# Reordering the start of the last stage of a fused attention and expert kernel, folding weights in three rounds, and swapping operands for its last token block

## The chip, the core and the metric

The kernel runs on one core of one Trainium2 chip. The metric is the device time of one execution in microseconds (us), the median of several executions. The engines are named as the profile names them: PE is TensorE (PEld its weight loads), ACT ScalarE, DVE VectorE, POOL GpSimd, and SP the queue that issues all transfers.

## The reference

Attention over 4 batches, 12 heads, 448 tokens and 64 columns gives `x` with 1792 rows (tokens) and 768 columns. A soft mixture of experts makes 32 slots out of all tokens, sends them through 8 small networks, and mixes the slot outputs back into every token. The last stage multiplies by one more pair of matrices with `h * cos(h)` between them.

```python
d = softmax over tokens of x @ phi          # 1792 x 32
slot_input = d.T @ x                        # 32 x 768
slot_out[e] = relu(slot_input[e] @ w1[e]) @ w2[e]
x2 = c @ slot_out                           # c: softmax over slots, 1792 x 32
h = x2 @ w_in                               # 768 x 2048, float64 numbers
out = (h * cos(h)) @ w_out                  # 2048 x 768, float64 numbers
```

## The kernel before, in words

The front part (attention, then the slots) takes the first half of the time and is the same instruction for instruction before and after. At its end come the slot outputs: groups of matmuls whose 256 result columns ACT copies from PSUM into `so`, PE transposes, and DVE copies into `soT` (the tile `dT` in the trace).

The last stage never forms `x2`. It cuts the 2048 inner columns into 16 chunks and, for each, **folds** the slot outputs into the weight chunk: `w_mm` (task `wm`, six matmuls of 128 columns a chunk, one for each 128 rows of `soT`, each written to one of four strips of 32 output partitions), `w_4` (ACT copies), `w_rep` (task `wr`, one matmul that adds the strips up), `w_s` (ACT) and `w_d` (task `wd`, DVE). `GRP` says which one or two chunks share a fold. The weights arrive as float64; each 768 KB load goes into one of four raw buffers and is **decoded** into float32 by four instructions: `dec_a` on ACT (task `a`) and `dec_l`, `dec_h`, `dec_s` on DVE (`l`, `h`, `s`). Loads are numbered j = 0, 1, 2, ... (even: `w_in`, odd: `w_out`); load j takes the raw buffer of load j - 4 and is issued (`ld`) when `s` of j - 4 is done. A chunk of `w_out` is then split into a high part (task `u`, ACT) and a remainder (task `v`, POOL or DVE).

The tokens are cut into three blocks of 512 and a last one of 256 columns. A **step** s is one pair of block and chunk; `SEQ` lists the 64 of them, the last block being the last 16. A step is a chain: `H` (PE, one matmul into bank 6 or 7), `Y` (ACT), `R` (DVE), `S` (ACT, sine), `G` (DVE, which frees the bank), `K` (ACT, high part), `L` (POOL, remainder), and then `B`: for each of six 128-row pieces of the output three product matmuls into that piece's own PSUM bank, with weights stationary and activations moving:

```python
o = bank[m][:, 0:n_(s)]
PE.matmul(o, lhsT=wh, rhs=gh, start=first, stop=False)
PE.matmul(o, lhsT=wl, rhs=gh, start=False, stop=False)
PE.matmul(o, lhsT=wh, rhs=gl, start=False, stop=last)
```

Step 0 runs its 18 products in three passes of six (`back0`): high weights first, then the weight remainder, then the activation remainder. At a block's last chunk `finish` (task `F`) copies or adds the bank into SBUF and, at chunk 15, issues the store.

What runs when is set by a planner in the kernel's own code: each of the tasks above has a duration, dependencies and a key; a list scheduler with these numbers writes out one fixed order per engine, and every engine then works strictly in that order. Matmuls on a constant tile (`keep_warm`, each two records of 128 columns) fill PE's order where the planner sees it idle before the first product.

Of the kernel before, what the change touches and what calls it, by code (L numbers as in the profile page):

```python
# [8 lines left out]
F32 = mybir.dt.float32  # L9
# [22 lines left out]
SAFE = 0.0  # L32
LA = .4
KD = 0.0
LD = False
KW = (0, 7, 2, 2)
PL = {23: 2, 24: 1}
CFG = {'rm': 2,
        'evx': 'D',
# [117 lines left out]
def moe_stack_kernel(ctx: ExitStack, tc: tile.TileContext, qk, v, cst, phi, w1, w2, w_in, w_out, out):  # L157
# [505 lines left out]
    def w_cols(c, u):  # L663

        if c < 12:
            return [(ar[f"hl{c}"], 768 * u, 0, 6)]
        t = [ar[f"hl{3 * (c - 12) + i}"] for i in range(3)]
        return [(t[0], 1536, 0, 4), (t[1], 1536, 4, 2)] if u == 0 else [(t[1], 1792, 0, 2), (t[2], 1536, 2, 4)]

# [95 lines left out]
    with tc.manual_schedule():  # L765
        for g in range(2):
# [115 lines left out]
    def back0(s, m):  # L882
# [3 lines left out]
        for m in range(6):  # L886
            fc = seq[0][1]
            PE.matmul(bank[m][:, 0:n_(0)], lhsT=w_blk(fc, int(k_ == 1), m), rhs=gl if k_ == 2 else gh, start=k_ == 0,
                      stop=k_ == 2 and seq[0][3])

    def finish(s, m, eng):
        blk, fc = seq[s][:2]
        o, ob = bank[m][:, 0:n_(s)], part(blk, m)[:, 0:n_(s)]
        if any(t[0] == blk and t[3] for t in seq[:s]):
            DVE.tensor_tensor(ob, o, ob, ALU.add)
        elif eng is DVE:
            DVE.tensor_copy(ob, o)
        else:
            ACT.activation(ob, o, AF.Copy)
        if fc == 15:  # L900
            SP.dma_start(out[128 * m:128 * m + 128, TOK[blk]:TOK[blk + 1]], ob)

# [29 lines left out]
    task(("so",), dict(DMA=5.199999999999999), [], -1)  # L932
    for q, grp in enumerate(GRP):
        key = need[grp[0]] - 1.5
        n = len(grp)
        task(("wm", q), dict(T=.3 + .45 * n), [("s", 2 * c) for c in grp if c] + [("w4", q - 2) if q >= 2 else None, ("so",)], key - .8)
# [4 lines left out]
    pb = {}  # L941
    for s, (blk, fc, first, last) in enumerate(seq):
        w = n_(s) / 512.0
# [4 lines left out]
        task(("G", s), dict(D=.07 + .54 * w), [("S", s)], s - 2.3)  # L948
        task(("K", s), dict(A=.1 + .46 * w), [("G", s), ("B", s - 4, 5) if s >= 4 else None], s - 1.7)
# [5 lines left out]
        for m in range(6):  # L955
            if s == 0:
# [3 lines left out]
                continue  # L960
            pv_ = ("B", s, m - 1) if m else (("B", s - 1, 5) if s else None)
            task(("B", s, m), dict(T=.01 + .67 * w), [("K", s), ("L", s), ("u", fc), ("v", fc), pv_, pb.get(m) if first else None], s + m / 10)
            if last:
                seen = any(t[0] == blk and t[3] for t in seq[:s])
                task(("F", s, m), dict(D=.07 + .54 * w) if seen or m % 2 == 0 else dict(A=.08 + .42 * w), [("B", s, m)], s + .2 + m / 10)
                pb[m] = ("F", s, m)
    LAT = dict(T=.24, A=.17, D=.1, P=.1, DMA=.9)
# [100 lines left out]
    with tc.manual_schedule():  # L1068
        for _, _, t, e in plan:
# [75 lines left out]
```

## Time and profile before

| | before |
|---|---|
| median of 3 runs | 527.82 us (527.72 to 528.99) |
| the profiled execution's own time | 532.41 us |
| span in the profile, first to last instruction | 530.6 us |
| PE, DVE, ACT, POOL busy | 498.8, 351.2, 310.5, 184.3 us |
| granted TensorE clock, mean | 0.986 of full speed |

The span is 1.8 us shorter than the profiled execution, and that execution is 4.6 us longer than the median of the runs without a profiler. The slot outputs end, and the last stage begins, near 248 us of the span. A matmul row's duration is longer than the distance to the next one's start, since matmuls overlap; what PE needs for one is read from start to start.

### The profile page before, as it was taken

Reading aid. Unit: us, or ns where it says so; the run is one execution under the profiler, and the core shown is the slowest. Engines: PE = TensorE matmul, PEld = TensorE weight load, DVE = VectorE, ACT = ScalarE, POOL = GpSimd, SP = SyncE. Lnnn points to the kernel's source line nnn. Section 1 sums busy time; section 2 is a strip of 40 time slices with the busy share of each in tenths; the row PEclk is TensorE's granted clock in tenths of the full one; section 3 lists DMA queues with packets and bytes.
Section 4 is the critical chain, followed back from the end, with each engine's and each line's share of the span. In section 5 each row is a group of like instructions: output and inputs, shape, how many; then the busy total and the mean of one; then the engine's idle time right before and its main releaser. Section 6 shows DMA issues by size and latency. Waiting matters only on the chain.

```text
span 530.6 us, 11216 instructions
## 1 busy us (share of the span) xinstructions
PE 498.8 (94%) x4292; PEld 364.7 (69%) x4292; DVE 351.2 (66%) x874; ACT 310.5 (59%) x734; POOL 184.3 (35%) x251
## 2 busy tenths in 40 slices
PE   6999999999999898886889999999999999999997
PEld 4676577576666633243767868787877777888996
DVE  3788688778767452003888899887997976445431
ACT  3899789779868121002769665747556546543552
POOL 0565356435445000000326333243434357222321
PEclk9899999989989999999899999999999999999999
DMA  5596767748658899999453423333163010213101
GB/s 193 176 324 225 272 216 254 256 164 299 210 179 319 309 416 422 421 419 417 160 192 107 153 86 119 120 117 122 63 225 105 26 61 24 95 40 131 69 1 61
DMA packets 24246, 100.38 MB, mean 189 GB/s; under 512 B 2816, under 2 KB 6912, under 8 KB 18048
## 3 DMA queue, kind: packets, MB, share of 16 engines
q1 hardware_dynamic: 24192, 99.66, 51.3%
q8 instruction: 34, 0.56, 0.4%
q14 instruction: 20, 0.16, 0.1%
HBM read 94.14 MB, written 5.51 MB: 188 GB/s over the span
## 4 chain that ended last, share of the span: by engine, by line
PE 55%; DVE 17%; DMA 16%; ACT 8%; issue 2%; POOL 1%; SPq 0%; ACTq 0%; POOLq 0%; DVEq 0%
PE bank L377 10%; PE bank L880 7%; PE bank L879 7%; PE bank L878 7%; PE bank L295 7%; DMA w<-in_w_dram 6%; PE bank L333 6%; DMA zraw<-in_w_out_dram 5%; DMA zraw<-in_w_in_dram 4%; DVE zscr L859 2%; ACT zraw L704 2%; DVE zscr L865 2%; ACT zscr L862 2%; PE bank L852 2%; DVE zhl L739 2%
## 5 line engine op out<-in xcount | busy, mean ns | idle before, releaser
L878 PE MATMUL bank<-zg,zhl 128*128 128x512 f32 (+1 forms) x378 | 139.7, 370 | 0.4 <-ACT zhl L726 0.4
L879 PE MATMUL bank<-zg,zhl 128*128 128x512 f32 (+1 forms) x378 | 137.5, 364 | 0.9 <-DVE zhl L739 0.9
L880 PE MATMUL bank<-zg,zhl 128*128 128x512 f32 (+1 forms) x378 | 137.3, 363 | 0.8 <-POOL zg L871 0.8
L871 POOL TENSOR_TENSOR zg<-zscr,zg 128x512 fp32r<-128x512 f32 (+1 forms) x64 | 82.7, 1297 | 140.3 <-ACT zg L868 127.3
L330 POOL TENSOR_SCALAR p<-p,pst 128x448 f32<-128x448 f32 (+3 forms) x168 | 81.5, 505 | 89.7 <-ACT pts L179 62.0
L313 ACT ACTIVATE p<-p,pst 128x448 f32<-128x448 f32 (+3 forms) x168 | 87.4, 521 | 22.1 <-DVE pst L311 22.1
L878 PEld LDWEIGHTS bank<-zg,zhl 128*128 128x128 f32 x378 | 71.5, 189 | 13.7 <-issue 1.2
L880 PEld LDWEIGHTS bank<-zg,zhl 128*128 128x128 f32 x378 | 71.4, 189 | 12.6 <-POOL zg L871 1.3
L879 PEld LDWEIGHTS bank<-zg,zhl 128*128 128x128 f32 x378 | 71.5, 189 | 12.4 <-DVE zhl L739 1.4
L862 ACT ACTIVATE zscr<-zscr,b_h 128x512 f32<-128x512 f32 (+1 forms) x64 | 42.0, 669 | 31.4 <-DVE zscr L859 31.3
L859 DVE SCALAR_TENSOR_TENSOR zscr<-zscr,bank 128x512 f32<-128x512 int32 (+1 forms) x64 | 38.7, 617 | 32.3 <-ACT zscr L856 31.9
L311 DVE CUSTOM_DVE_ANT_0 p<-bank,cs 128x448 f32<-128x448 f32 (+1 forms) x96 | 50.7, 547 | 10.8 <-PE bank L295 10.8
L295 PE MATMUL bank<-qk 64*128 64x192 f32 (+2 forms) x288 | 55.6, 462 | 0.6 <-ACT xk L179 0.5
L868 ACT ACTIVATE zg<-zscr 128x512 fp32r<-128x512 f32 (+1 forms) x64 | 36.3, 575 | 26.0 <-DVE zscr L865 25.9
L865 DVE TENSOR_TENSOR zscr<-bank,zscr 128x512 f32<-128x512 f32 (+1 forms) x64 | 39.1, 620 | 18.3 <-ACT zscr L862 18.3
L856 ACT ACTIVATE zscr<-bank,b_q 128x512 int32<-128x512 f32 (+1 forms) x64 | 39.4, 629 | 19.2 <-PE bank L852 19.0
L739 POOL TENSOR_TENSOR zhl<-uacc,zhl 128x768 fp32r<-128x768 f32 (+1 forms) x7 | 10.8, 1552 | 99.9 <-DMA zraw<-in_w_out_dram 84.8
L704 ACT ACTIVATE zraw<-zraw 128x768 f32<-128x768 f32 x32 | 29.2, 912 | 25.7 <-DMA zraw<-in_w_in_dram 14.6
L181 DVE COPY pts<-bank 128x512 f32<-128x512 f32 x48 | 33.0, 687 | 12.3 <-PE bank L333 12.0
L333 PE MATMUL bank<-cs,p 64*128 64x64 f32 (+1 forms) x768 | 34.7, 228 | 1.3 <-POOL p L330 1.0
L333 PEld LDWEIGHTS bank<-cs,p 64*128 64x128 f32 (+1 forms) x768 | 28.6, 135 | 7.0 <-POOL p L330 3.9
L179 ACT ACTIVATE pts<-bank 128x512 f32<-128x512 f32 x48 | 28.0, 584 | 8.1 <-PE bank L333 7.6
(143 smaller groups left out, 709.2 us busy)
## 6 DMA issues: line engine op xcount, KB each, us to landing
w<-in_w_dram SPq DMA_DIRECT2D x48, 1024.0 KB, 8.0
zraw<-in_w_in_dram SPq DMA_DIRECT2D x16, 768.0 KB, 4.5
zraw<-in_w_out_dram SPq DMA_DIRECT2D x16, 768.0 KB, 4.4
qk<-in_qk_dram SPq DMA_DIRECT2D x24, 480.0 KB, 3.6
xk<-in_v_dram SPq DMA_DIRECT2D x12, 256.0 KB, 4.7
out_dram<-zps SPq DMA_DIRECT2D x8, 256.0 KB, 2.0
xts<-in_v_dram SPq DMA_DIRECT2D x12, 128.0 KB, 3.5
lt<-in_v_dram SPq DMA_DIRECT2D x12, 128.0 KB, 4.1
```

The source lines that it names most:

```text
L295: PE.matmul(sreg(j, c), lhsT=Q(p)[h, q0:q0 + 128], rhs=K(p)[h, 0:ln], start=True, stop=True)
L311: DVE.tensor_tensor_reduce(out=dst, in0=sb, in1=m, scale=-0.125, scalar=3.0e38, op0=ALU.add, op1=ALU.min, accum_out=st_[:, col:col + 1])
L313: return pr(f"exp{j}{c}")(lambda: ACT.activation(dst, dst, AF.Exp, bias=st_[:, col:col + 1], scale=-1.0, accum_out=st_[:, 8 + col:9 + col]))
L330: ENG[CFG["norm"][3 * j + c if c < 3 else 6]].tensor_scalar(dst, dst, st_[:, 24 + col:25 + col], 0.0, op0=ALU.mult, op1=ALU.add)
L333: PE.transpose(out, src, by)
L377: PE.matmul(OB[64 * j:64 * j + 64, a:b], lhsT=V(p, c, j), rhs=r[j], start=first, stop=last)
L862: ACT.activation(y_(s), y_(s), AF.Sin, bias=b_h, scale=1.0)
L865: DVE.tensor_tensor(y_(s), hb[:, 0:n_(s)], y_(s), ALU.mult)
L871: eng.tensor_tensor(g_(s)[1], y_(s), g_(s)[0].bitcast(F32), ALU.subtract)
L878: PE.matmul(o, lhsT=wh, rhs=gh, start=first, stop=False)
L879: PE.matmul(o, lhsT=wl, rhs=gh, start=False, stop=False)
L880: PE.matmul(o, lhsT=wh, rhs=gl, start=False, stop=last)
```

## The change

Four things are edited; all lie after the 248th microsecond.

- **Slot outputs first.** The copy into `so` and the copy into `soT` stand ahead of the decoding of load 1 on ACT and on DVE instead of behind it, with one more `keep_warm` ahead of the transposes and two behind the second copy.
- **Fold in three rounds.** Where a fold has two chunks, its twelve `wm` matmuls are dealt over the four strips so that no strip gets more than three; before, two strips got four.
- **Last block with activations stationary.** `back3` replaces `back` in the last 16 steps: the activations are `lhsT` (two groups of 128 tokens), the weight chunk is the moving operand, and the output is not transposed. A step's 18 matmuls of 256 columns become 6 of 512 and 6 of 256, in three units that take banks 0, 2, and 1 with 3. `finish3` replaces six copies and six stores of 128 KB by two copies of 512 columns, two of 256, and three stores of 256 KB.
- **A new order.** 52 keys of the planner are shifted (`KEYS`), three `v` tasks are put on a named engine (`VE`), and some of its durations and starting times are altered.

```diff
-LA = .4
+LA = 0.3
+KEYS = {
+    ('B', 10, 2): 7.75, ('B', 12, 5): 3.75, ('B', 13, 3): 1, ('B', 14, 3): 8.75, ('B', 18, 2): 2, ('B', 18, 4): 5.25,
...
+VE = {0: 'D', 3: 'P', 8: 'D'}
...
-                if npc[0] == 48:
-                    decode(1)
                 ACT.activation(so, sb[:, 0:256], AF.Copy)
                 tb = bank[6]
                 if npc[0] == 48:
-                    keep_warm(1)
+                    keep_warm(2)
+                    dec_a(1)
...
+                if npc[0] == 48:
+                    keep_warm(2)
+                    dec_l(1)
+                    dec_h(1)
+                    dec_s(1)
...
     def w_mm(q, wb):
-        for k_, n in enumerate(GRP[q]):
-            for ch in range(6):
-                r = ch % 4
-                PE.matmul(wb[32 * r:32 * r + 32, 128 * k_:128 * k_ + 128], lhsT=soT[:, ch, :],
-                          rhs=fwi(n)[:, 128 * ch:128 * ch + 128], start=(ch < 4), stop=(ch + 4 >= 6))
+
+        ts = [(0, 0, 0), (0, 1, 1), (0, 2, 2), (0, 3, 3), (0, 4, 0), (0, 5, 1)]
+        if len(GRP[q]) == 2:
+            ts += [(1, 0, 2), (1, 1, 3), (1, 2, 2), (1, 3, 3), (1, 4, 0), (1, 5, 1)]
+        seen = set()
+        for x, (k_, ch, r) in enumerate(ts):
+            PE.matmul(wb[32 * r:32 * r + 32, 128 * k_:128 * k_ + 128], lhsT=soT[:, ch, :],
+                      rhs=fwi(GRP[q][k_])[:, 128 * ch:128 * ch + 128], start=(k_, r) not in seen,
+                      stop=not any(y[0] == k_ and y[2] == r for y in ts[x + 1:]))
+            seen.add((k_, r))
...
+    U3 = (((0, 0, 512, 0),), ((1, 0, 512, 2),), ((0, 512, 768, 1), (1, 512, 768, 3)))
...
+    def back3(s, k):
+
+        blk, fc, first, last = seq[s]
+        gh, gl = g_(s)
+        for k_, a, b, bn in U3[k]:
+            ob = bank[bn][:, 0:b - a]
+            th, tl = (g[:, 128 * k_:128 * k_ + 128] for g in (gh, gl))
+            wh, wl = w_seg(fc, 0, a, b), w_seg(fc, 1, a, b)
+            PE.matmul(ob, lhsT=th, rhs=wh, start=first, stop=False)
+            PE.matmul(ob, lhsT=th, rhs=wl, start=False, stop=False)
+            PE.matmul(ob, lhsT=tl, rhs=wh, start=False, stop=last)
+
+    def finish3(k, eng):
+        o3 = out[DM * TOK[3]:DM * NT].rearrange("(t p c) -> p t c", t=2, p=128)
+        if k < 2:
+            ob = ar["ps"][:, 512 * k:512 * k + 512]
+            copy("D" if eng is DVE else "A", ob, bank[(0, 2)[k]])
+            SP.dma_start(o3[:, k, 0:512], ob)
+            return
+        ob = ar["ps"][:, 1024:1536]
+        DVE.tensor_copy(ob[:, 0:256], bank[1][:, 0:256])
+        ACT.activation(ob[:, 256:512], bank[3][:, 0:256], AF.Copy)
+        SP.dma_start(o3[:, :, 512:768], ob.rearrange("p (t c) -> p t c", t=2))
...
-    free = dict(T=6.0, A=5.6, D=5.95, P=3.0)
+    free = dict(T=3.6, A=3.95, D=6.05, P=3.0)
```

How the instructions stand is shown at three places; line numbers differ between the two files.

**ACT, at the end of the slot outputs.** `cs<-bank_68 128x256` is the copy into `so`, `zraw_2734` to `zraw_2737` are `dec_a` of loads 0 to 3, `cs<-bank_70` is `w_4` and `zWS` is `w_s` of the first fold. Before:

```order
L704 ACTIVATE zraw_2734<-zraw_2734 128x768
L704 ACTIVATE zraw_2735<-zraw_2735 128x768
L798 ACTIVATE cs<-bank_68 128x256
L704 ACTIVATE zraw_2736<-zraw_2736 128x768
L827 ACTIVATE cs<-bank_70 128x128
L704 ACTIVATE zraw_2737<-zraw_2737 128x768
L834 ACTIVATE zWS<-bank_70 96x128
```

and now:

```order
L714 ACTIVATE zraw_2734<-zraw_2734 128x768
L806 ACTIVATE cs<-bank_68 128x256
L714 ACTIVATE zraw_2735<-zraw_2735 128x768
L847 ACTIVATE cs<-bank_70 128x128
L714 ACTIVATE zraw_2736<-zraw_2736 128x768
L854 ACTIVATE zWS<-bank_70 96x128
```

The copy moved ahead of `dec_a` of load 1; `dec_a` of load 2 now stands between the first fold's two ACT copies.

**PE, from the second fold on.** `zfa,dT` and `zfb,dT` are `wm`, `cs 96x...` is `wr`, `CT,zWS` is `H`, `cs 128x128` is `keep_warm`, `zg,zhl` are products. Before, the second fold and `H` of steps 0 (the row just ahead), 1 and 2 all stand ahead of the first product:

```order
L852 MATMUL bank_70<-CT,zWS 128x512
L819 MATMUL bank_71<-zfa,dT 32x128 x6
L467 MATMUL bank_67<-cs 128x128 x2
L830 MATMUL bank_71<-cs 96x128
L467 MATMUL bank_67<-cs 128x128 x6
L852 MATMUL bank_70<-CT,zWS 128x512
L852 MATMUL bank_71<-CT,zWS 128x512
L888 MATMUL bank_64<-zg_3072,zhl_3075 128x512
```

Now the 18 products of step 0 come first (after 17 `keep_warm`), with `wm` of the second fold between the second and the third pass. What stands between the last of them and the first product of step 1 is this:

```order
L908 MATMUL bank_69<-zg_3075,zhl_3078 128x512
L850 MATMUL bank_70<-cs 96x128
L872 MATMUL bank_70<-CT,zWS 128x512
L872 MATMUL bank_71<-CT,zWS 128x512
L872 MATMUL bank_70<-CT,zWS 128x512
L837 MATMUL bank_71<-zfb,dT 32x128 x12
L898 MATMUL bank_64<-zg_3075,zhl_3079 128x512
```

`wr` of the second fold, `H` of steps 1, 2 and 3 and `wm` of the third fold moved from both sides into the place between step 0 and step 1.

**DVE, around `G` of step 0.** `zscr<-bank_70,zscr` is `G`, `zWS` is `wd` of the second fold, the rows on `zraw` are decoding (`TENSOR_SCALAR` is `l`, the first `SCALAR_TENSOR_TENSOR` on a load is `h`, the second `s`), `zhl` is `v`. Before:

```order
L865 TENSOR_TENSOR zscr<-bank_70,zscr 128x512
L838 TENSOR_TENSOR zWS<-bank_71,zWS 32x128
L711 SCALAR_TENSOR_TENSOR lt<-zraw_2737,lt 128x768
L859 SCALAR_TENSOR_TENSOR zscr<-zscr,bank_70 128x512
L859 SCALAR_TENSOR_TENSOR zscr<-zscr,bank_71 128x512
L707 TENSOR_SCALAR zfb<-zraw_2736 128x768
```

and now:

```order
L885 TENSOR_TENSOR zscr<-bank_70,zscr 128x512
L749 TENSOR_TENSOR zhl_3078<-uacc,zhl_3078 128x768
L725 SCALAR_TENSOR_TENSOR zfa<-zraw_2736,zfa 128x768
L717 TENSOR_SCALAR zfb<-zraw_2734 128x768
L721 SCALAR_TENSOR_TENSOR zfb<-zraw_2734,zfb 128x768
L721 SCALAR_TENSOR_TENSOR lt<-zraw_2737,lt 128x768
L725 SCALAR_TENSOR_TENSOR lt<-zraw_2737,lt 128x768
L717 TENSOR_SCALAR zfb<-zraw_2736 128x768
L858 TENSOR_TENSOR zWS<-bank_70,zWS 32x128
L725 SCALAR_TENSOR_TENSOR zfb<-zraw_2734,zfb 128x768
```

`v` of chunk 0 came from POOL to DVE, and `wd` of the second fold fell from the row behind `G` to eight rows behind it, right after `l` of load 6 (the second use of `zraw_2736`).

Farther on, `wr` of the later folds moved away from their `wm`: the third fold had 3 product matmuls between the two and has 18, the fourth had 3 and has 18, the fifth had 3 and has 45; and of the undivided `v` tasks of chunks 1 to 11 six stood on DVE before (chunks 1, 4, 6, 7, 9, 11) and three stand there now (5, 8, 11).

## Rows read from the trace of the kernel before

**Rows 1.** PE's waits from 266 us to the end: us in total, times, longest.

```profile
PE bank L852 <- DVE zscr L865: 1.7, 3, 0.9
PE bank L852 <- DVE zWS L838: 1.5, 2, 0.8
PE bank L879 <- DVE zhl L739: 0.9, 1, 0.9
PE bank L830 <- ACT cs L827: 0.9, 2, 0.5
PE bank L880 <- POOL zg L871: 0.8, 1, 0.8
```

**Rows 2.** PE's timeline, 247 to 275 us: start, us, what, idle before.

```profile
247.76 1.05 PE L792 MATMUL bank<-w,dk 128*4 128x256 f32 x16 [0.58 <-DMA w<-in_w_dram]
...
250.86 0.44 PE L803 MATMUL bank<-cs 128*128 128x128 f32 x2 [1.63 <-ACT cs L798]
252.68 1.07 PE L819 MATMUL bank<-zfa,dT 128*32 128x128 f32 x12 [1.38 <-DVE dT L804]
...
255.12 1.28 PE L467 MATMUL bank<-cs 128*128 128x128 f32 x6
256.16 0.48 PE L852 MATMUL bank<-CT,zWS 96*128 96x512 f32 x1
256.57 0.63 PE L819 MATMUL bank<-zfa,dT 128*32 128x128 f32 x12
...
257.93 1.50 PE L467 MATMUL bank<-cs 128*128 128x128 f32 x12
...
260.51 4.26 PE L888 MATMUL bank<-zg,zhl 128*128 128x512 f32 x18
...
266.80 0.50 PE L879 MATMUL bank<-zg,zhl 128*128 128x512 f32 x1 [0.94 <-DVE zhl L739]
...
273.86 1.07 PE L819 MATMUL bank<-zfb,dT 128*32 128x128 f32 x24
```

**Rows 3.** ACT's timeline, 249 to 253 us.

```profile
249.63 0.90 ACT L704 ACTIVATE zraw<-zraw 128x768 f32<-128x768 f32 x1 [8.99 <-DMA zraw<-in_w_out_dram]
250.44 0.37 ACT L798 ACTIVATE cs<-bank 128x256 f32<-128x256 f32 x1
251.52 0.95 ACT L704 ACTIVATE zraw<-zraw 128x768 f32<-128x768 f32 x1 [0.72 <-DMA zraw<-in_w_in_dram]
```

**Rows 4.** DVE's timeline, 252 to 267 us.

```profile
252.44 0.18 DVE L804 COPY dT<-bank 128x32 f32<-128x32 f32 x1
252.54 0.55 DVE L707 TENSOR_SCALAR zfa<-zraw 128x768 int32<-128x768 int32 x1
...
254.19 0.96 DVE L715 SCALAR_TENSOR_TENSOR zfa<-zraw,zfa 128x768 int32<-128x768 int32 x1
...
265.34 1.40 DVE L739 TENSOR_TENSOR zhl<-lt,zhl 128x768 fp32r<-128x768 f32 x1 [0.32 <-ACT zhl L726]
```

**Rows 5.** Stretches of 1 us: busy us of PE, PEld, DVE, ACT, POOL; then PEclk.

```profile
253.00:254.00 1.00, 1.00 (x13) 0.59 (x6) 0.90 (x2) 0.21 (x2) 0.00 (x0) 0.50 0.84 221
...
256.00:257.00 1.00, 1.00 (x16) 0.68 (x15) 0.55 (x1) 0.70 (x2) 0.55 (x1) 0.97 0.91 227
```

**Rows 6.** All 32 weight loads (line 697): issue to landing.

```profile
DMA to landing us min/median/max: 4.0/4.4/19.2
```

**Rows 7.** PE's timeline: a run of 512-column, then of 256-column products.

```profile
487.81 0.40 PE L878 MATMUL bank<-zg,zhl 128*128 128x512 f32 x1
...
490.54 0.28 PE L878 MATMUL bank<-zg,zhl 128*128 128x256 f32 x1
...
526.53 0.28 PE L880 MATMUL bank<-zg,zhl 128*128 128x256 f32 x1
```

**Rows 8.** The end: timeline, and the last store's issue and landing.

```profile
528.02 0.40 SPq L901 DMA_DIRECT2D out_dram<-ctok  x1
...
out_dram<-ctok SPq DMA_DIRECT2D x1, 128.0 KB, 1.8
```

More of the change, by code (lines that the diff above doesn't have):

```diff
@@ L667, in w_cols @@
         t = [ar[f"hl{3 * (c - 12) + i}"] for i in range(3)]
-        return [(t[0], 1536, 0, 4), (t[1], 1536, 4, 2)] if u == 0 else [(t[1], 1792, 0, 2), (t[2], 1536, 2, 4)]
+        return [(t[0], 1536, 0, 4), (t[1], 1536, 4, 2)] if u == 0 else [(t[2], 1536, 0, 4), (t[1], 1792, 4, 2)]
     def w_blk(c, u, m):
@@ L809, in moe_stack_kernel @@
     WS, scr = ar["WS"], ar["scr"]
+    oT = out[0:DM * TOK[3]].rearrange("(d t) -> d t", d=DM)
     def w4(q):
@@ L889, in back0, with w_seg @@
                       stop=k_ == 2 and seq[0][3])
+    U3 = (((0, 0, 512, 0),), ((1, 0, 512, 2),), ((0, 512, 768, 1), (1, 512, 768, 3)))
+    def w_seg(fc, u, a, b):
+        for t, o, m0, nm in w_cols(fc, u):
+            if 128 * m0 <= a and b <= 128 * (m0 + nm):
+                return t[:, o + a - 128 * m0:o + b - 128 * m0]
+    def back3(s, k):
[19 more added lines that the diff above has]
+        SP.dma_start(o3[:, :, 512:768], ob.rearrange("p (t c) -> p t c", t=2))
     def finish(s, m, eng):
@@ L900, in finish @@
         if fc == 15:
-            SP.dma_start(out[128 * m:128 * m + 128, TOK[blk]:TOK[blk + 1]], ob)
+            SP.dma_start(oT[128 * m:128 * m + 128, TOK[blk]:TOK[blk + 1]], ob)
     T = {}
@@ L935, in moe_stack_kernel @@
         n = len(grp)
-        task(("wm", q), dict(T=.3 + .45 * n), [("s", 2 * c) for c in grp if c] + [("w4", q - 2) if q >= 2 else None, ("so",)], key - .8)
+        task(("wm", q), dict(T=.3 + .22 * (n + 1)), [("s", 2 * c) for c in grp if c] + [("w4", q - 2) if q >= 2 else None, ("so",)], key - .8)
         task(("w4", q), dict(A=.15 + .11 * n), [("wm", q)] + [("wr", q - 2) if q >= 2 else None], key - .7)
@@ L941, in moe_stack_kernel, with nu @@
     pb = {}
+    def nu(s):
+        return 3 if seq[s][0] == 3 else 6
     for s, (blk, fc, first, last) in enumerate(seq):
@@ L948, in moe_stack_kernel @@
         task(("G", s), dict(D=.07 + .54 * w), [("S", s)], s - 2.3)
-        task(("K", s), dict(A=.1 + .46 * w), [("G", s), ("B", s - 4, 5) if s >= 4 else None], s - 1.7)
+        task(("K", s), dict(A=.1 + .46 * w), [("G", s), ("B", s - 4, nu(s - 4) - 1) if s >= 4 else None], s - 1.7)
         task(("L", s), dict(P=.07 + 1.2 * w, D=.07 + .55 * w) if LD else dict(P=.07 + 1.2 * w), [("K", s)], s - 1.5, True)
@@ L954, in moe_stack_kernel @@
             task(("B", 0, 5), dict(T=1.4), [("B", 0, 1), ("L", 0)], .2)
-        for m in range(6):
+        for m in range(nu(s)):
             if s == 0:
@@ L960, in moe_stack_kernel @@
                 continue
-            pv_ = ("B", s, m - 1) if m else (("B", s - 1, 5) if s else None)
+            pv_ = ("B", s, m - 1) if m else (("B", s - 1, nu(s - 1) - 1) if s else None)
+            if blk == 3:
+                task(("B", s, m), dict(T=(.68, .68, .73)[m]), [("K", s), ("L", s), ("u", fc), ("v", fc), pv_, *([pb.get(x) for x in ((0,), (2,), (1, 3))[m]] if first else [])], s + m / 10)
+                if last:
+                    task(("F", s, m), (dict(D=.61), dict(A=.5), dict(D=.35))[m], [("B", s, m)], s + .2 + m / 10)
+                continue
             task(("B", s, m), dict(T=.01 + .67 * w), [("K", s), ("L", s), ("u", fc), ("v", fc), pv_, pb.get(m) if first else None], s + m / 10)
@@ L966, in moe_stack_kernel @@
                 pb[m] = ("F", s, m)
+    for t, x in KEYS.items():
+        T[t] = T[t][:2] + (T[t][2] + x,) + T[t][3:]
+    for c, e in VE.items():
+        T["v", c] = ({e: T["v", c][0][e]},) + T["v", c][1:]
     LAT = dict(T=.24, A=.17, D=.1, P=.1, DMA=.9)
@@ L1062, in moe_stack_kernel @@
     bk = lambda t: bank[6 + hbo[t]]
-    run = dict(ld=ld, a=dec_a, l=dec_l, h=dec_h, s=dec_s, u=up_part, S=t_s, K=t_k, B=lambda s, m: (back if s else back0)(s, m))
+    run = dict(ld=ld, a=dec_a, l=dec_l, h=dec_h, s=dec_s, u=up_part, S=t_s, K=t_k, B=lambda s, m: (back3 if seq[s][0] == 3 else back if s else back0)(s, m))
     run.update(H=lambda s: t_h(s, bk(("H", s))), Y=lambda s: t_y(s, bk(("H", s))), R=lambda s: t_r(s, bk(("H", s))),
@@ L1079, in moe_stack_kernel @@
             elif t[0] == "F":
-                finish(t[1], t[2], ENG[e])
+                finish3(t[2], ENG[e]) if seq[t[1]][0] == 3 else finish(t[1], t[2], ENG[e])
             else:
@@ L1136 @@
         args.append(nc.dram_tensor(f"in_{name}_dram", a.shape, mybir.dt.from_np(a.dtype), kind="ExternalInput").ap())
-    args.append(nc.dram_tensor("out_0_dram", (DM, NT), F32, kind="ExternalOutput").ap())
+    args.append(nc.dram_tensor("out_0_dram", (DM * NT,), F32, kind="ExternalOutput").ap())
     with tile.TileContext(nc) as tc:
```

6 lines of the change are left out of this document (4 added, 2 removed), and 7 rows, old and new, of the table KEYS.

## The prediction

> **What bounds the kernel now.** I read the granted clock and PE's share first (0.986 and 498.8 of 530.6 us, in the table above), then PE's waits in the last stage, then the timelines where the stage begins and ends. PE is the engine to account for: from 266 us to the end it waits nine times for 5.8 us in all [rows 1], and everything else there is matmuls in one unbroken row. So an edit in this part pays if it shortens PE's own work or takes one of these waits away. A wait's row counts from the end of a matmul, and that end is modelled: a 512-column product is given 0.40 us, but a row of twelve of them, from 487.81 to 490.54, goes at 2.73 / 12 = 0.2275 us each [rows 7]. A wait therefore costs about 0.17 us more than it shows. Without the one on line 879, which belongs to the start, eight waits of 4.9 us are left, worth 4.9 + 8 x 0.17 = 6.3 us.
>
> The start is the other place. The last slot matmuls end at 248.8, PE's transposes begin at 250.86 after 1.63 us of idling, and the first fold at 252.68 after 1.38 more [rows 2]. The reader should see why: ACT copies the slot outputs only at 250.44, since the decoding of load 1, which landed at 249.6, stands ahead of it in ACT's order [rows 3], and DVE's copy comes at 252.44, behind three decoding instructions [rows 4]. It has a second price: in 253 to 254 the clock is at half, 1.2 GHz, and it is back to 2.4 GHz in the microsecond from 256 [rows 5]. The constant matmuls show it too: six records take 1.28 us at 255.12 and twelve 1.50 us at 257.93, 0.21 against 0.125 us each [rows 2]. About 3.3 us, 252.7 to 256.0, pass at half speed.
>
> **The start, step by step.** The copy into `so` can now run at 248.85 and takes 0.37 us [rows 3], the transposes 0.44 [rows 2], the copy into `soT` 0.18 [rows 4]: the first fold starts at 249.9 instead of 252.68, 2.8 us sooner. A fold of one chunk takes 0.63 us at full clock [rows 2]. From its end to `H` of step 0 it was 253.75 to 256.16, 2.4 us; I keep that, because `dec_a` of load 2 now stands in the middle, and that load lands at 251.5 and occupies ACT to 252.4 [rows 3]. `H` is at 253.0, and the first product, 4.35 us behind it as before (256.16 to 260.51), at 257.3: 3.2 us sooner. The 17 `keep_warm` are 34 records x 0.125 = 4.25 us and fit under this chain at full clock. The decoding and `v` that moved into it on ACT and DVE fill waits of the chain; `v` of chunk 0 is needed only by the second pass, 1.4 us into the products.
>
> What comes behind the products is worse than before. The 18 products take 18 x 0.2275 = 4.1 us, the second fold's `wm` 0.6, its `wr` 0.3 (two records, like a `keep_warm`): PE is through at 262.3 and needs `wd` of that fold. DVE's order decides when. `H` to first product has five links of about 0.7 us (`Y`, `R`, `S`, `G`, `K`), so `G` of step 0 ends at 256.6. Then come `v`, 1.40 us at its only clear example, and `s` of load 2, 0.96 [rows 4]: 259.0. Only then load 6 can be issued into the same raw buffer. A load takes 4.4 us from issue to landing [rows 6]: 263.4. `l` of load 6, 0.55 us [rows 4], stands ahead of `wd`, so DVE is held by a transfer with the chain queued behind it. `wd`, behind it, ends near 264.3, and `H` of steps 1 and 2 run. `R` of step 1 is behind two more decoding instructions, 2 x 0.96: 266.2. `R`, `S`, `G` end at 268.3, `s` of load 6 at 269.3, `G` of step 2 at 270.0. That frees bank 7 for the third fold, 0.8 us, which stands ahead of step 1's products in PE's order: they start at 270.8. Before, step 1 ran unbroken from 266.80 - 0.23 = 266.57 [rows 2], and the third fold came later and cost 1.0. **The start loses** 270.8 - 266.57 - 1.0 = 3.2 us. In the 8.5 us from 262.3 PE works for about two; before its slow stretch it had done little but two transposes since 248.8. I take it that the clock falls again and that 3.3 us of products run at half speed: 1.6 us more. The bounds are nothing (clock stays) and 3.3 / 2 + 0.4 for the fold.
>
> **Folds.** `wm` of two chunks, four rounds, lasts 1.07 us and of one chunk, two rounds, 0.63 [rows 2]: 0.22 a round. Six further folds lose one round each: 1.3 us gained, nothing where PE waits beside it.
>
> **Last block.** From 490.54 to 526.53 there are 301 records (288 products and 13 `H`): 35.99 / 300 = 0.120 us each [rows 7]. A step had 18 x 0.120 = 2.16 us of products and has 6 x 0.2275 + 6 x 0.120 = 2.085. Over 16 steps 1.2 us are gained. The bounds: nothing, if a product of 512 columns with activations stationary goes no faster per column than one of 256, and 2.4 us, if those of 256 go at the 512's pace per column.
>
> The Trainium skill, "TensorE: Matmul & The Clock Gate", section "Back-to-back issue gap", gives the distance of isolated matmuls at full clock as columns over 2.4 plus 2.5 ns: 216 and 109 ns. By that rule, an estimate from that page, a step would go from 1.97 to 1.95 us and the block would gain 0.2 us. The trace has 227.5 and 120 ns, and the price per matmul that these imply is larger; I go by the rows.
>
> **End.** The last product ends at 526.8, the last store is issued at 528.02, behind five others, and lands 1.8 us later [rows 8]. With three stores SP is free when the last copies end, 0.5 us after the last product: 0.7 us gained, less about 0.4 for twice the bytes in the last store. I take 0.3; bounds nothing and 0.7.
>
> **The waits after the start.** The order is new from end to end, so none of the eight old waits need recur, and each new one costs the same kind of price. Bounds: nothing, and the old 6.3. Two PE waits were for ACT's copy of a fold, 0.9 us [rows 1]; with 18 or more products between `wm` and `wr` instead of 3 these have cover (18 x 0.2275 = 4.1 us). Three were for DVE's `wd` or POOL's remainder, 2.3 us, while decoding was late; the later start of step 1 leaves decoding some 3 us ahead, and DVE has three `v` of later chunks fewer. What stands as before is an `H` that needs the bank which an earlier `G` frees: three waits, 1.7 us. I take 1.7, the row it is nearest to.
>
> **Sum** against the profile's own span of 530.6 us: +3.2 +1.6 -1.3 -1.2 -0.3 -6.3 +1.7 = -2.6. The profiled execution, 532.41, is 4.6 us above the median of the runs; I carry the difference over to the median: 527.8 - 2.6 = **525.2 us**.
>
> **Rivals.**
> - *Shorter hole.* The clock holds, and step 1 starts 0.7 us sooner (`v` on DVE takes less than the 1.40 us, which was measured beside a working POOL): -4.9, 522.9 us. For it: gaps of 0.58 us between slot matmuls left the clock alone. Against: the hole is longer than the gaps that lowered it.
> - *Slower: the waits recur.* Loads that land behind an engine's head, with chain instructions queued behind them, hold PE in the new order for as long as in the old, 6.3 us. The sum is then +2.0, 529.8 us; it is slower beyond 0.3% once the new waits pass 5.9 us. For it: the hole is such a case already, and five of the old waits were DVE's. Against: loads 7, 8 and 10 can be issued earlier than before.
> - *The start gains nothing.* The clock falls at the slot outputs all the same; 34 records x 0.21 = 7.1 us then hold the first product to about 260.6. The hole shrinks, since load 6 does not wait for PE; its chain starts 0.8 us later: 526.0.
> - *The page's rule holds* for the last block: 1.0 us less gain, 526.2 us.
>
> **Numbers.** A change under 0.3%, 1.6 us, is about what a measurement of this kernel cannot tell from none; the limits are 526.2 and 529.4 us. Forecast 0.45 (its own range, with waits of 0 to 3.3 us, is 523.5 to 526.8), shorter hole 0.25, waits recur 0.17, no gain at the start 0.08, the page's rule 0.05. Faster: four fifths of the first, all of the second, some of the last two: 0.69. Slower: two thirds of the recurring waits: 0.11. Same: 0.20. Leaving out a tenth on each side, the range is 521.3 (no new wait at all and a short hole would be 521.2) to 528.6.
>
> **What would show it.** In the new trace: the first fold at 249.9 and the first product near 257.3 at full clock; `wd` of the second fold ending near 264.3 right behind `l` of load 6, which waits for its transfer; no product between 262.3 and about 270.8, and half clock after it; `wm` of two chunks at 0.85 us instead of 1.07; last-block steps of 2.2 us with `H`; the last store issued 0.5 us after the last product. The prediction is wrong if the hole is under 4 us long, or if PE's waits after it sum to more than 4 us.

## The result: slower, and the profile after

The changed kernel takes 534.57 us (median of 13 runs, 531.02 to 537.35). The kernel before, run on the same chips, takes 528.99 (13 runs, 526.40 to 535.86). The ratio is 1.0119, with an interval of 1.0094 to 1.0145: 5.0 to 7.7 us slower, outside the predicted range. The profiled execution of the changed kernel took 533.31 us, its span is 531.5 and its mean clock 0.990.

**A common zero.** The front part, the same instructions in every kernel here, ended its last slot matmul anywhere from 243.6 to 252.0 us in 17 profiles. That end goes with the time for which the granted clock was at half (1.2 GHz) ahead of it: 243.6 us in the one profile with none, 245.5 to 246.8 in nine with 3.4 us, among them after, 247.4 to 248.8 in four with 10.2 us, among them before, and 251.4 to 252.0 in three with 17.1 us. What comes after it repeats much more closely. So from here on times are also counted from S, the end of the last slot matmul: 248.81 before [rows 2], 246.11 after. Counted so, the last product ends at 278.00 before and 280.71 after, and the tail from there to the end of the span is 3.82 and 4.71 us: 3.6 us lost in all. A second profile of the kernel before gave 276.99 and 3.90; against that one 4.5 us are lost. The rest of the timed 5.0 to 7.7 us was not located.

PE's timeline of the changed kernel, from `H` of step 0 to the third fold (start, us, what, idle before), shows the start:

```profile
250.28 0.50 PE L872 MATMUL bank<-CT,zWS 96*128 96x512 f32 x1 [0.41 <-DVE zWS L858]
250.62 3.96 PE L477 MATMUL bank<-cs 128*128 128x128 f32 x34
254.42 3.02 PE L908 MATMUL bank<-zg,zhl 128*128 128x512 f32 x12
...
259.45 0.38 PE L850 MATMUL bank<-cs 128*96 128x128 f32 x2
261.87 0.73 PE L872 MATMUL bank<-CT,zWS 96*128 96x512 f32 x2 [2.04 <-DVE zWS L858]
265.92 0.80 PE L872 MATMUL bank<-CT,zWS 96*128 96x512 f32 x1 [3.32 <-DVE zscr L885]
267.39 1.51 PE L837 MATMUL bank<-zfb,dT 128*32 128x128 f32 x24 [0.67 <-DVE zscr L885]
```

Step 0 runs at S + 8.31 instead of 11.70, 3.4 us sooner, at full clock. Then PE stands: three waits of 6.0 us between 259.8 and 267.4, all for DVE, and step 1 starts at 268.83, S + 22.72. Windows of 2 us (busy us of PE, PEld, DVE, ACT, POOL, then the clock) show what follows:

```profile
264.00:266.00 2.00, 0.08 (x1) 0.08 (x1) 1.81 (x4) 1.43 (x3) 1.34 (x1) 0.59 0.87 313
266.00:268.00 2.00, 1.33 (x13) 0.79 (x17) 1.80 (x3) 1.72 (x3) 1.27 (x1) 0.50 0.55 115
268.00:270.00 2.00, 2.00 (x23) 1.40 (x15) 1.68 (x4) 2.00 (x5) 1.08 (x1) 0.50 0.71 283
...
272.00:274.00 2.00, 2.00 (x11) 1.61 (x10) 1.07 (x3) 1.72 (x4) 1.20 (x1) 1.00 0.00 0
```

The granted clock falls to half (1.2 GHz) at 264.4 us, while PE stands, and is back at 271.2: the third fold takes 1.51 us where the later two-chunk folds, at full clock (2.4 GHz), take 0.86, and the first products of step 1 go at 0.43 us from start to start. DVE is busy 1.7 to 1.8 of every 2 us up to 270. Its timeline, 253 to 262 us:

```profile
253.62 0.95 DVE L749 TENSOR_TENSOR zhl<-uacc,zhl 128x768 fp32r<-128x768 f32 x1
254.49 2.07 DVE L725 SCALAR_TENSOR_TENSOR zfa<-zraw,zfa 128x768 int32<-128x768 int32 x1
...
260.93 0.56 DVE L717 TENSOR_SCALAR zfb<-zraw 128x768 int32<-128x768 int32 x1 [0.98 <-DMA zraw<-in_w_in_dram]
261.52 0.29 DVE L858 TENSOR_TENSOR zWS<-bank,zWS 32x128 fp32r<-32x128 f32 x1
```

`v` takes 0.95 us here, `s` of load 2 takes 2.07, load 6 is waited for 0.98 us, and `wd` (L858) comes right behind its `l`, as predicted. PE's waits from 259 us to the end (us in total, times, longest), which answer to [rows 1]:

```profile
PE bank L872 <- DVE zscr L885: 6.1, 5, 3.3
PE bank L872 <- DVE zWS L858: 4.6, 4, 2.0
PE bank L837 <- DVE zscr L885: 0.7, 1, 0.7
PE bank L898 <- DVE zps L948: 0.6, 1, 0.6
```

Every one is a wait for DVE. They sum to 12.0 us; 6.0 are the three of the stretch in which PE stands, called the hole from here on, and 6.0, in eight waits, come later. The longest of those, 1.61 us, ends at 331.19, and DVE's timeline ahead of it shows what such a wait is made of:

```profile
323.42 0.64 DVE L717 TENSOR_SCALAR lt<-zraw 128x768 int32<-128x768 int32 x1 [0.93 <-DMA zraw<-in_w_out_dram]
324.30 0.96 DVE L721 SCALAR_TENSOR_TENSOR lt<-zraw,lt 128x768 int32<-128x768 int32 x1 [0.24 <-ACT zraw L714]
325.30 1.93 DVE L725 SCALAR_TENSOR_TENSOR lt<-zraw,lt 128x768 int32<-128x768 int32 x1
327.15 2.47 DVE L946 TENSOR_TENSOR zraw<-bank,zraw 128x512 f32<-128x512 f32 x4
...
330.71 0.42 DVE L858 TENSOR_TENSOR zWS<-bank,zWS 32x256 fp32r<-32x256 f32 x1
```

A load that lands late, a decoding instruction at twice its length, then bank additions and more decoding, and only then the 0.42 us of `wd` that PE needs.

### The profile page after: what moved, and what is told of

Its sections match the earlier page's. It is cut to its first block, busy times and chain, and to the rows that moved or that the text cites. A ratio compares the mean times of both kernels' runs of the same rounds, so it can differ in the third digit from the quotient of the medians.

```text
span 531.5 us, 11076 instructions
## 1 busy us (share of the span) xinstructions
PE 496.3 (93%) x4222; PEld 360.4 (68%) x4222; DVE 349.6 (66%) x868; ACT 310.2 (58%) x733; POOL 189.5 (36%) x252
## 4 chain that ended last, share of the span: by engine, by line
PE 66%; DVE 17%; DMA 8%; ACT 5%; issue 2%; POOL 1%; ACTq 0%; SPq 0%; POOLq 0%; DVEq 0%
PE bank L387 9%; PE bank L898 7%; PE bank L305 7%; PE bank L899 7%; PE bank L900 7%; PE bank L343 6%; DMA zraw<-in_w_in_dram 5%; PE bank L787 4%; DMA zraw<-in_w_out_dram 3%; PE bank L802 3%; PE bank L926 2%; PE bank L927 2%; PE bank L928 2%; PE bank L872 2%; DVE zscr L885 2%
## 5 line engine op out<-in xcount | busy, mean ns | idle before, releaser
L898 PE MATMUL bank<-zg,zhl 128*128 128x512 f32 x282 | 112.8, 400 | 0.6 <-DVE zps L948 0.6
L899 PE MATMUL bank<-zg,zhl 128*128 128x512 f32 x282 | 110.6, 392 | 0.0
L900 PE MATMUL bank<-zg,zhl 128*128 128x512 f32 x282 | 110.4, 391 | 0.0
L898 PEld LDWEIGHTS bank<-zg,zhl 128*128 128x128 f32 x282 | 53.3, 189 | 13.6 <-issue 1.6
L900 PEld LDWEIGHTS bank<-zg,zhl 128*128 128x128 f32 x282 | 53.2, 189 | 11.6
L899 PEld LDWEIGHTS bank<-zg,zhl 128*128 128x128 f32 x282 | 53.4, 189 | 11.0
L872 PE MATMUL bank<-CT,zWS 96*128 96x512 f32 (+1 forms) x64 | 24.1, 389 | 11.1 <-DVE zscr L885 6.1
```

## The experiments

All milestones were read from the timelines, in us, and are starts of steps counted from S; "last" is the end of the last product, counted the same way, and "tail" the rest of the span behind it. Each ratio is to runs of the kernel before on the same chip.

| kernel | step 2 | step 14 | step 48 | last | tail | ratio to before |
|---|---|---|---|---|---|---|
| before | 22.12 | 83.09 | 241.73 | 278.00 | 3.82 | |
| before_again | 22.15 | 82.85 | 240.71 | 276.99 | 3.90 | 1.0021 (0.9988 to 1.0054) |
| after | 28.31 | 89.08 | 245.22 | 280.71 | 4.71 | 1.0119 (1.0094 to 1.0145) |
| parts_old_order | 22.28 | 82.91 | 241.01 | 276.48 | 4.71 | 1.0052 (1.0015 to 1.0090) |
| last_block_only | 21.97 | 82.98 | 240.59 | 276.05 | 4.71 | 1.0003 (0.9975 to 1.0032) |
| hole_closed | 27.25 | 90.54 | 246.99 | 282.48 | 4.71 | 1.0103 (1.0062 to 1.0143) |
| after_warm | 26.56 | 88.35 | 245.11 | 280.60 | 4.71 | 1.0085 (1.0053 to 1.0117) |
| hole_closed_warm | 25.15 | 88.95 | 245.31 | 280.79 | 4.72 | 1.0107 (1.0062 to 1.0151) |
| after_no_s | 27.33 | 83.20 | 235.89 | 271.38 | 3.88 | work left out |
| before_no_s | 22.12 | 80.36 | 235.64 | 271.91 | 3.70 | work left out |
| after_short_loads | 27.63 | 86.67 | 240.62 | 276.11 | 4.71 | work left out |
| after_pool_short | 28.06 | 86.45 | 243.25 | 278.74 | 3.88 | work left out |
| after_tail | 28.06 | 88.90 | 245.55 | 281.02 | 4.06 | 1.0080 (1.0048 to 1.0112) |
| old_order_tail | 22.64 | 83.34 | 240.86 | 276.31 | 4.45 | 0.9980 (0.9955 to 1.0005) |
| f_copies_old | 22.42 | 81.72 | 239.70 | 275.14 | 3.64 | 0.9958 (0.9923 to 0.9992) |
| f_copies_old_one | 22.02 | 81.72 | 240.01 | 275.46 | 3.65 | 0.9940 (0.9906 to 0.9973) |
| f_copies_new | 28.39 | 87.80 | 244.49 | 279.98 | 3.88 | 1.0086 (1.0045 to 1.0126) |

**Parts without the order.** `before_again` is the kernel before, unedited.

> The kernel before, unchanged, to see how much one profile of it differs from the next. All theories expect a ratio of 1.00 within 0.4%. If the 2.7 us by which the slot outputs ended sooner in the changed kernel's profile is scatter, they end anywhere between 246 and 249 us here, and the stretch from their end to the last product is 278.0 us within 1 us.

> The three edits (slot outputs first, folds in three rounds, last block with activations stationary) in the old order; step 1 to 63 stand as before. Theory A, the new order is what costs: first fold 2.8 us sooner, step 1 some 2 us sooner, folds 1.5 us, last block 1.2 us, last store up to 0.9 us later: 2.5 to 4 us faster than before, ratio 0.992 to 0.996. Rival B, the edits themselves cost (the store at the end, or the operands swapped): not faster than before, ratio 1.000 or more.

`parts_old_order` has every part of the change but the new order. Against the changed kernel, in excerpts:

```diff
-LA = 0.3
+LA = .4
-KEYS = {
...
-VE = {0: 'D', 3: 'P', 8: 'D'}
...
-    free = dict(T=3.6, A=3.95, D=6.05, P=3.0)
+    free = dict(T=6.0, A=5.6, D=5.95, P=3.0)
```

> The kernel before with the last block's operands swapped and its three stores, nothing else; the order is the old one. Theory A: products 1.2 us shorter (a step 2.2 us instead of 2.28 with H), the last store lands about 0.9 us later: 0.3 us faster, ratio 0.999 to 1.000. Rival B: the swap itself slows the block or its end, ratio 1.003 or more.

`last_block_only` has `back3`, `finish3` and nothing else of the change; its ratio of 1.0003 cannot be told from none. In the profiles the same parts end 4.2 us sooner in the old order than in the new one (276.48 against 280.71), so counted from S the loss is the order's. The timing agrees in part: `parts_old_order` was expected at 0.992 to 0.996 and is at 1.0052, slower than before, though its profile from S to the end of the span is 0.6 us shorter than one profile of before and 0.3 us longer than the other. By the ratios the order costs 0.67%, some 3.5 us, and the parts the other 0.5%; where the parts lose that was not located. Taking the copy into `so` early gains nothing there: the first fold starts 2.5 us sooner, but the first product at 11.85 instead of 11.70, since `wd` still stands behind the decoding of load 2 on DVE.

**Closing the hole by hand.** `hole_closed` puts the tasks of the stretch in an order that takes `wd` of the second fold ahead of the decoding of load 6, and the third fold into step 1 (excerpt):

```diff
+    O = [("h", 3), ("w4", 1), ("s", 3), ("wr", 1), ("ld", 7), ("ws", 1), ("wd", 1), ("s", 4), ("H", 1), ("u", 1), ("H", 2),
...
+    plan[:] = plan[:i] + [at[t] for t in O] + [x for x in plan[i:] if x[2] not in O]
```

> The changed kernel with its order altered between step 0 and step 1 alone: wd of the second fold, R, S and G of steps 1 and 2 stand ahead of the decoding of load 6, and the third fold behind three blocks of step 1. Theory A: the hole behind step 0's products shrinks from 9.3 to some 5 us, and 3 to 4 us of the 6 us lost come back (ratio to before 1.004 to 1.006). Rival C, the hole is paid back anyway because decoding is what limits the next 60 us: the hole shrinks, the waits after it grow by as much, ratio stays 1.010 to 1.013.

Step 1 starts at 18.74 instead of 22.72, and step 2 at 27.25 instead of 28.31: of 4.0 us 1.1 are left one step later, in part because the third fold now stands inside step 1 and still takes 1.51 us at half clock. At step 13 it is 0.3 us ahead (82.32 against 82.61); behind the wait there, 1.78 us against 1.61 in `after`, the clock falls to half from 337.6 to 341.0 us, which it does not in `after`, and the last product comes 1.8 us later. That second fall was seen in one profile, so no more is read from the end than that the gain is gone; the ratio, 1.0103, agrees with the rival. Two windows behind the hole show the clock:

```profile
272.00:274.00 2.00, 2.00 (x6) 1.56 (x5) 1.97 (x4) 0.90 (x3) 1.18 (x1) 0.50 0.02 9
274.00:276.00 2.00, 2.00 (x26) 1.08 (x25) 2.00 (x4) 0.56 (x1) 0.35 (x1) 0.50 0.80 255
```

**Holding the clock.** Matmuls on constants, or on zeros added to a bank, fill the hole (excerpt, the largest of the three groups):

```diff
+            if t == ("H", 3):
+                for _ in range(12):
+                    PE.matmul(bank[3][:, 0:128], lhsT=z_, rhs=cs[:, 0:128], start=False, stop=False)
```

> The changed kernel with matmuls on constants in PE's hole between step 0 and step 1 (7 ahead of H of step 1, 12 that add zeros ahead of H of step 3, 2 ahead of the third fold, each 0.23 us at full clock), so that PE does not idle there; nothing else is changed. Theory: the hole costs twice, by its length and by the half clock behind it. Then the clock stays at 1.00 through the third fold and step 1, the fold takes 0.85 us instead of 1.51, the products of step 1 go at 0.2275 us from the first on, step 2 starts 1.7 to 1.9 us sooner counted from the last slot matmul, and the last product comes at 278.9 instead of 280.7 on that count. Rival 1: what comes behind (decoding on DVE and ACT, loads) sets the pace of the steps after the hole; the gain at step 2 is there but by step 10 PE waits for it again and the last product stays within 0.5 us of 280.7. Rival 2: matmuls on constants do not hold the clock; nothing moves.

> The kernel whose hole was closed to some 5 us by hand, with matmuls on constants in what is left of the hole (2 ahead of H of step 1, 11 that add zeros ahead of H of step 3). Theory: the 4 us won at step 1 were given back because nine products and the third fold ran at half clock; then the last product moves from 282.5 to about 279.7 counted from the last slot matmul, and the third fold takes 0.85 instead of 1.51 us. Rival: the third fold and step 2 wait for decoding whatever the clock; then step 2 starts within 0.7 us of 27.25 as before, and the last product stays above 281.5.

The clock holds in `after_warm`:

```profile
266.00:268.00 2.00, 1.46 (x25) 1.23 (x29) 2.00 (x4) 2.00 (x3) 1.28 (x1) 1.00 0.39 115
```

Step 2 starts 1.75 us sooner, as the theory said, and 1.6 us of it are left at step 13. Then it is waited away: 0.7 us in one wait (2.35 instead of 1.62) ahead of step 14, nearly all of it by step 30, and the last product gains 0.11 us. Rival 1 holds, only later than step 10: something other than PE sets the pace. `hole_closed_warm` gains 1.7 us of the 2.8 expected, lies between its two expectations, and ends where `after` does; behind a wait of 2.3 us in step 2 the granted clock fell to half all the same, from 277.1 to 280.5 us.

**What sets the pace.** Each of four kernels leaves something out, as its expectation says; their outputs are therefore other numbers, and their times serve only here.

> The changed kernel without the third decoding instruction (the sign bits) of loads 4 to 31, which leaves that part of the decoding out: 28 instructions of 0.96 us, 27 us less work for DVE, nothing less for PE. Theory: DVE, not PE, sets the pace from the slot outputs to about step 38 (it is over 90% busy there), and PE's waits behind the hole are waits for DVE's backlog. Then PE's waits after step 1, 6.0 us now, fall below 1.5, and the last product comes at 275.5 or sooner, counted from the last slot matmul, instead of 280.7. Rival: the transfers are late, whatever DVE does; then more than 4 us of waits stay and the last product comes at 279 or later.

> The kernel before with the same instructions left out. Theory: its 4.9 us of waits behind the start were DVE's too; the last product comes at 273 to 274 instead of 278.0 (277.0 in its second profile), and the distance to the changed kernel with the same cut is what the start costs less what folds and last block gain, 1.5 to 3 us. Rival: PE sets the pace of the kernel before; its last product stays within 1 us of 277 to 278.

```diff
     def dec_s(j):
+        if j >= 4:
+            return
```

PE's waits of `after_no_s` from S + 13 to the end:

```profile
PE bank L874 <- DVE zscr L887: 2.9, 1, 2.9
PE bank L874 <- DVE zWS L860: 2.0, 1, 2.0
```

These are the two of the hole; all later ones are gone, and the last product comes 9.3 us sooner. The kernel before gains 6.1 us by the same cut (5.1 against its second profile). Both theories hold: the decoding on DVE holds both kernels back, and the new order more. The distance between the two was expected at 1.5 to 3 us and is -0.5: with DVE relieved, the changed kernel makes good all but 0.25 of its 5.2 us at the start by step 48 and ends ahead. The cut does two things at once, though: it frees DVE, and a load that follows into a raw buffer no longer waits for `s`.

> The changed kernel with loads 4 to 31 bringing only the first quarter of each weight block, so that most of the decoded numbers are stale; every instruction is kept. A load should land in some 2.5 instead of 4.3 us. Theory (DVE sets the pace): most waits stay, the last product comes at 279 or later, for a load is late only at single places (one each behind 256, 316 and 355 us on the chain that ended last). Rival (transfers set it): PE's waits after step 1 fall below 2 us and the last product comes at 276.5 or sooner.

> The changed kernel with POOL's activation remainder (L) of steps 4 to 63 cut to 64 columns, which leaves the rest of the remainders stale: POOL is busy for some 55 us less in the last stage. Theory: DVE's decoding instructions take 0.95 us alone and up to 2.5 us where POOL works at the same time, 16 us more in all up to step 38 than at 0.95 and 0.55 us each; much of that goes, DVE ends its decoding sooner, PE's waits after step 1 fall by 3 us or more, and the last product comes at 278 or sooner instead of 280.7. Rival: POOL does not slow DVE, or only where DVE has time; the last product stays within 0.7 us of 280.7.

```diff
-        SP.dma_start(raw(j), ...)
+        n = 1536 if j < 4 else 384
+        SP.dma_start(raw(j)[:, 0:n], ...[:, 0:n])
```

The theory for `after_short_loads` failed and its rival nearly holds: loads that land in 2.4 us (median) instead of 4.5 gain 4.6 us at the last product. Its waits are

```profile
PE bank L873 <- DVE zscr L886: 4.8, 4, 3.3
PE bank L873 <- DVE zWS L859: 1.4, 2, 1.0
PE bank L838 <- DVE zscr L886: 0.7, 1, 0.7
PE bank L899 <- DVE zps L949: 0.6, 1, 0.6
```

7.5 us with 5.0 in the hole, so 2.5 later instead of 6.0. The transfer belongs to DVE's loop: a load is issued when DVE has finished the one four places back, and a DVE that is nine tenths full has little time to make up for a landing that it waits for. So it is the loop of DVE and its loads that sets the pace, and how the two share it was not separated. With the lighter POOL 2.0 us are gained, between theory and rival, and the waits after step 1 do not fall as much as expected (4.2 us stay).

**Work moved off DVE, nothing left out.** In the old order with folds, last block and the end by units (next paragraph), first copies of output banks go from DVE to ACT; this is the edit for three of them, with `(0, 2, 4)` for nine:

```diff
+                e = "A" if t[1] in (1, 4, 8) and t[2] in (4,) else e
```

> The old order with folds in three rounds, the new last block and its last two steps by units (last product at 276.3 counted from the last slot matmul), and with the nine first copies of output banks that DVE made (steps 1, 4 and 8, 0.68 us each) made by ACT at the same places of the order; nothing is left out. Theory: DVE sets the pace up to about step 36, so 6.1 us less DVE work show as 1 to 3 us of PE's waits, most of it by step 10, and the last product comes at 275.3 or sooner. Rival: ACT is as full as DVE there (39 of 47 us busy) and its chain instructions now stand behind the copies; the last product comes at 276 or later.

> The same with only one of the three copies of each of these steps moved to ACT, 2.0 us of DVE work. Theory: 0.3 to 1 us gained, last product at 275.3 to 276.0. Rival: ACT's queue behind the copies costs what DVE wins; 276.0 to 276.8.

> The changed kernel with the nine copies on ACT, nothing else changed. Theory (DVE sets the pace of the new order): PE's waits after step 1 fall by 1.5 us or more, and the last product comes at 279.2 or sooner instead of 280.7. Rival (the loads and the order of decoding set it, ACT has no room): the last product stays at 280.2 or later.

Moving three copies (2.0 us of DVE) brings the last product from 276.31 to 275.46, moving nine to 275.14, 0.9 and 1.2 us. The timed difference between these two is inside their intervals. Either beats the kernel before: 0.9940 and 0.9958. In the new order the nine copies give 0.7 us, between the two expectations, and PE's waits from 259 us on fall from 12.0 to 11.4 us and not by 1.5: DVE's time alone is not the whole of it. ACT, which the expectation had 39 of 47 us busy, was busy 35.36 us of the 47 from S + 13 on in the kernel before. The Trainium skill, "Perfetto Trace Analysis", section "Optimizing Scalar/DVE Operations", says that work that either engine can do may be better on ScalarE when DVE is saturated; the trace agrees here, to the extent of these numbers.

**The tail.**

> The changed kernel with the products of the last two steps in another order: both steps' products of the first unit, then of the second, then of the third, so that the copy and the store of a unit come 2.8, 1.4 and 0 us ahead of the last product instead of 1.4, 0.7 and 0. Theory: the tail is long (4.71 us from the last product to the end, 3.82 before) because three stores of 256 KB are issued within 1.1 us and the last one's packets stand behind the others'; a store of 256 KB alone landed in 2.0 us, so the tail shrinks to about 3.5 us. Rival: the last store's own size and its straggling packets set it; the tail stays at 4.5 us or more.

> The kernel before, in its own order, with the fold in three rounds, the last block with activations stationary, and the last two steps' products by units as in the other kernel of this batch; the slot outputs stay behind the decoding of load 1. Theory: these are the two parts of the change that pay by themselves: folds 0.7 us, last block 0.8 us, and the tail at 3.5 instead of 3.82: 1.8 us under before in the profile, a ratio near 0.9965. Rival: the tail stays at 4.7 us; then only 0.6 us are left and the ratio is 0.999 or above.

```diff
+    O = [t for m, f in zip((0, 1, 2), (0, 1, 2)) for t in (("B", 62, m), ("B", 63, m), ("F", 63, f))]
```

The tail is 4.06 us in `after_tail` (4.71 without the edit) and 4.45 in `old_order_tail`; the theories had 3.5. The ratio of `old_order_tail`, 0.9980 (0.9955 to 1.0005), lies between its two expectations and cannot be told from none. What the tails have in common is another thing. The DMA view of `after` from 527.2 us on, and of `f_copies_new`, with the same three stores, from 526 us on:

```profile
q1 hardware_dynamic: 525, 0.71, 46.6%
q14 instruction: 1, 0.01, 0.4%
issues: line engine op xcount, KB each, median us to landing
out_dram<-zps SPq DMA_DIRECT2D x1, 256.0 KB, 3.2
```

```profile
q1 hardware_dynamic: 539, 0.74, 58.0%
issues: line engine op xcount, KB each, median us to landing
out_dram<-zps SPq DMA_DIRECT2D x1, 256.0 KB, 2.4
```

In `after` one packet of 8 KB, program code, falls among the last store's; the store lands in 3.2 instead of 2.4 us, and the tail is 4.71 instead of 3.88. All nine profiles with a code packet in their last 2.8 us have tails of 4.06 to 4.72, the other eight 3.64 to 3.90 (the two of before have such a packet earlier, 4.4 to 4.5 us from the end). Of the kernels that end by units, `after_tail` and `old_order_tail` have it (4.06, 4.45) and the two `f_copies_old` have not (3.64, 3.65), which may be part of their better ratios. That the packet does it is not shown: it was seen in this sorting and not tried by itself.

## Why the prediction was wrong

- **The step that failed is "The waits after the start".** I took 1.7 us for the new waits against 6.3 of the old. Measured by the distance between starts of matmuls over the usual one, the eight old ones after the start cost 6.8 us in the trace of before, the new ones 7.9 between steps 1 and 48. The term -6.3 + 1.7 is +1.1: 5.7 us off, most of the miss. The prediction's own sign of being wrong, more than 4 us of waits behind the hole, is met with 6.0. The reason behind the term was wrong too: "the later start of step 1 leaves decoding some 3 us ahead". It was not ahead: all eight new waits are for DVE, and they are gone where `s` of loads 4 to 31 is left out (`after_no_s`). I had called PE the engine to account for, from its 94% share of the whole span, and had not looked at DVE's share of this stretch. The windows from S + 13 to S + 60 and on to S + 125 (DVE is the third engine) give, for the kernel before,

```profile
261.80:308.80 47.00, 43.91 (x223) 33.25 (x222) 41.23 (x57) 35.36 (x56) 18.08 (x13) 1.00 0.39 135
308.80:373.80 65.00, 63.39 (x313) 50.37 (x312) 57.20 (x77) 40.81 (x63) 24.25 (x16) 1.00 0.32 110
```

and for the changed kernel

```profile
259.10:306.10 47.00, 38.82 (x196) 29.23 (x195) 42.76 (x56) 33.96 (x55) 22.01 (x14) 0.93 0.39 131
306.10:371.10 65.00, 61.53 (x306) 48.61 (x305) 55.34 (x74) 38.86 (x60) 26.28 (x17) 1.00 0.40 139
```

At 85 to 91% (my expectations said over 90), with chains and transfers to wait for, DVE has little time to make good. Counting its rows from S on shows what the order does to it: ahead of `G` of step 10 stand 29 decoding instructions before and 33 after; ahead of `G` of step 30 there are 78 and 84, which take 74.5 and 81.0 us. More decoding stands ahead of the same step, and the chain that PE waits for stands behind it. The rival "the waits recur" had this mechanism, with 0.17; its 529.8 us was too low as well.
- **"The start, step by step" was right.** First fold at S + 1.38 and first product at S + 8.31 (forecast S + 1.1 and 8.5, from S = 248.8), half clock after the hole, step 1 at S + 22.72 (forecast 22.0). Step 1, less the 1.0 us of the third fold, came 4.0 us later than its unbroken start before (S + 17.76), and half clock inside it cost 1.2, together 5.2 us against 3.2 + 1.6. Links were off both ways: `v` 0.95 instead of 1.40, `s` of load 2 2.07 instead of 0.96. The rival "shorter hole" would have gained little: 4 us of hole were closed and 1.75 us of clock won in the experiments, and both were gone by step 48.
- **"Folds" held, but bought little.** A two-chunk fold is 0.21 us shorter (0.86 instead of 1.07), as forecast; with the folds, step 48 of `parts_old_order` comes 0.7 us sooner than in one profile of before and 0.3 later than in the other. What PE saves while it waits for DVE it waits away.
- **"Last block" was right in sign, mis-sized.** Steps 48 to the end take 35.49 us instead of 36.27: 0.8 us, not 1.2. Its products go at 0.234 and 0.119 us from start to start, so a step needs 2.12 us where I took 2.085. The upper bound of 2.4 us was summed wrongly: 6 x 0.2275 + 6 x 0.114 gives 1.8. By the rule that the prediction quotes from the Trainium skill, "TensorE: Matmul & The Clock Gate", section "Back-to-back issue gap", the gain was an estimate of 0.2 us; this trace does not agree, and the rule is further off than my rows.
- **"End": wrong sign.** Copies and issue came as forecast, 0.45 us after the last product, but the store took 3.2 us to land, and the tail grew by 0.9 us where I took -0.3. The 0.4 us that I took off for twice the bytes had no row behind it; in `f_copies_new`, without the code packet, a last store of that size lands in 2.4 us, 0.6 more than the 1.8 of [rows 8].

With these terms the sum is 5.2 + 1.1 - 1.3 - 0.8 + 0.9 = 5.1 us. The profiles differ by 3.6 and 4.5, so 1.5 and 0.6 us are assigned to no term. The milestones say where the loss lies: at step 2 the changed kernel is 6.2 us behind, and from there to step 48 it takes 216.9 us, against 219.6 and 218.6 before. It wins some of the start back, but not the 6.3 us of old waits that I had struck out.

## What to carry to other kernels

Read each engine's busy share by stage, not over the span: the engine with the longest row in the whole kernel need not be the one that sets the pace where the change is. Here a side engine was nine tenths full: time won on the main engine was waited away, and instructions put ahead of the chain held it back, needed soon or not. Relief of that engine, or of the loads that it waits for, is what paid: with copies given to ACT, the old order with folds, last block and the end by units has the lowest ratios of this study, 0.9940 with three copies and 0.9958 with nine, which are not told apart.

## What the runs showed of the hardware

- DVE's decoding instruction `s` takes 0.95 us alone and, from 254.49 us on, 2.07 beside a POOL instruction that ran from 254.45 for 1.29 us, about the two in turn. The Trainium skill, "SBUF — State Buffer", section "Who interferes with whom", says that a DVE instruction with two SBUF inputs and a GpSimd instruction that reads SBUF block each other whole; this row agrees.
- With matmuls on constants and on zeros in the hole (`after_warm`) the granted clock stayed at 1.00, 2.4 GHz, from 264 to 272 us; without them (`after`) it was at 0.50, 1.2 GHz, from 264.4 to 271.2.
- One 8 KB code packet among the last stores goes with 0.8 us more of tail with the same three stores (4.71 against 3.88 us); the cause was not tried.
- The identical front part ends anywhere within 8.4 us from profile to profile, later the longer the granted clock is at half in it (none: 243.6 us; 17.1 us: 251.4 to 252.0).
